# Where the seven-product chain keeps its PSUM banks, which product comes sixth, and when q and k are placed

## The chip, the cores and the metric

The kernel runs on one core of a Trainium2 chip. The metric is the device time of one launch in microseconds (us). The kernel before takes 352.87 us, the median of three runs (352.79 to 353.57). One more execution was taken with the hardware profiler; it has a time of its own, given below.

## The reference

Two stages follow each other. The first is causal attention with a forget gate, for 8 batches and 8 heads of 576 positions with 64 dimensions. The second is a two-layer MLP on the 4608 rows that attention gives, 512 wide, with 2048 hidden units and h - tanh(h) between the layers.

```python
scores = scale * np.matmul(q, k.transpose(0, 1, 3, 2))
cum = np.cumsum(np.log(np.clip(f, 0.0001, 1.0)), axis=-1)
decay = cum[:, :, :, None] - cum[:, :, None, :]
scores = np.where(causal, -1000000000.0, scores + decay)
attn = softmax(scores)                       # over the last axis
x = np.matmul(attn, v)                       # heads side by side: 4608 x 512
h = x @ w_in                                 # 4608 x 2048
out = (h - np.tanh(h)) @ w_out               # 4608 x 512, float32
```

## The kernel before

**Attention.** Batch 0 is done in an order written out by hand. From batch 1 on the work goes pair of heads by pair of heads: pair p is heads 2c and 2c+1 of batch b, with p = 4b + c, and each pair has a *slot*. A slot has seven score tiles, s0 to s6 (`scores`, L338): TensorE writes a tile of transposed scores into one of two PSUM banks of the pool `ps_sc`, ScalarE takes the exponential into SBUF, and from batch 2 on GpSimd sets the masked part to zero. `values` (L371) of the pair before comes behind the second tile of a slot: 30 products with v, then VectorE divides by the row sums into `xn`. `turn` (L389) sends `xn` with two DMA transposes on SyncE's queue into `XR`, which holds the input of the MLP with the hidden dimension on the partitions.

**How q and k come in.** They must stand with the head dimension on the partitions, in `QT` and `KT`, one buffer for even batches and one for odd ones. For batches 1 and 2 the raw rows are loaded as one long transfer for each of q and k (L205; those of batch 2 are issued in slot 4), and TensorE transposes them (`trans`, L236) pair by pair, one slot ahead: the transposes of q behind s0, those of k behind s3. Their PSUM tile has the only bank of the pool `ps_tr` (k of batch 1 is in `ps_m`), and VectorE copies it out. From batch 3 on, GpSimd's queue loads blocks (`load_block`, L92), SyncE's queue turns them by DMA (`turn_block`, L101) into `TQ` and `TK`, and then two more transfers each put the two halves into place (`place`, L105: a = 0 for the even heads, a = 1 for the odd ones). With p0 = 4(b-1), the transposes of q are issued in slot p0, those of k in slot p0+1, the two places of q in slot p0+2 behind s0 and s2, and those of k in slot p0+3 behind s0 and s2. The batch's own first slot is p0+4. The list `LOADS` (L209 to L227) holds all this. SyncE takes its queue in order.

**The MLP.** It works in units of 512 rows, nine in all. `mlp1` (L431) makes the hidden values of a unit in 16 steps: four matmuls of 512 columns into one of three banks of the pool `ps_m`, tanh on ScalarE, the sum on VectorE. Units 0 and 1 then have 16 plain steps of the second layer (`mlp2`). Units 2 to 8 use a scheme with seven half-size products in place of eight (`seven`, L509): 14 steps, each one product of eight matmuls of 256 columns for one half m of the columns. Products 0, 2, 4 and 5 add up in one running sum, called the chain, whose PSUM tile is `cx`. ScalarE copies the chain out behind products 0, 2, 4 and 5 (`keep`, into P1, U2, u3 and ost); products 1, 3 and 6 have tiles of their own and VectorE adds them (`add`, L486) to what was kept; `store` sends four quarters of the unit's output from SyncE's queue. VectorE also makes sums of the hidden values that serve as operands (`sums`, `more_sums`); those for product 6 are emitted in steps 5 and 7.

In units 2 to 5 the products come in their order 0 to 6: product 3 opens the tile `cy` and product 6 adds to the same tile, so that U2 needs one addition. In units 6 to 8 (`spare`) product 6 comes ahead of product 5, in a tile `cw` of its own, and U2 is added to twice. The chain has a bank of `ps_m`, product 1 that of `ps_tr`.

**What sets the order.** All five engines run their instructions in the order in which the program emits them. `slot` (L625) goes through the items of a slot and, after each, emits as many MLP steps as the slot's share `TAKE` has reached by then. In slot 7, where the share is 3, a step comes behind `values`, s4 and s6 instead. One exception is `held` (L616): step 10 of `seven`, which is product 5 on the chain just copied out, waits in units 2 to 5 until enough attention work was emitted since the last step:

```python
    def held():
        fn, _, s = mlp[done[0]]
        return fn is seven and s == 10 and since[0] < 0.85
```

Of the kernel before, what the change touches and what calls it, by code (L numbers as in the profile page):

```python
# [8 lines left out]
FP32 = mybir.dt.float32  # L9
# [8 lines left out]
FAR = 3  # L18
# [4 lines left out]
def kernel(  # L23
# [11 lines left out]
    P = 128  # L35
# [6 lines left out]
    NPAIR = H // 2  # L42
# [8 lines left out]
    UW = 512  # L51
    SB = UW // 2
    NU = NT // UW
# [9 lines left out]
    ps_sc = ctx.enter_context(tc.tile_pool(name="ps_sc", bufs=2, space=PSUM))  # L63
    ps_av = ctx.enter_context(tc.tile_pool(name="ps_av", bufs=1, space=PSUM))
    ps_tr = ctx.enter_context(tc.tile_pool(name="ps_tr", bufs=1, space=PSUM))
    ps_m = ctx.enter_context(tc.tile_pool(name="ps_m", bufs=3, space=PSUM))
# [25 lines left out]
    def load_block(dst, src, b, n, h0=0, h1=H):  # L92
        pn = min(P, S - n * P)
        nc.gpsimd.dma_start(out=dst[0:pn, n, h0:h1, 0:D], in_=src[b, h0:h1, n * P:n * P + pn, :].rearrange("h p d -> p h d"))  # L94
# [10 lines left out]
    def place(dst, src, b, a):  # L105
        nc.sync.dma_start(out=dst[b % 2][0:D, a:H:2, 0:S], in_=src[a * D:(a + 1) * D, :, :])

    def load_v(b, n):
        load_block(vn[b % 2], v, b, n)

    def raw_of(b):
        return 1 if b == FAR else 0
# [46 lines left out]
    def load_aug(b):  # L159
        i, h0 = b % 2, b * H  # L160
        nc.sync.dma_start(out=KT[i][D:D + 1, :, 0:S], in_=chi[h0:h0 + H, :])
        nc.sync.dma_start(out=QT[i][D + 2:D + 3, :, :], in_=cq[h0:h0 + H, :])
        nc.sync.dma_start(out=KT[i][D + 1:D + 2, :, 0:S], in_=clo[h0:h0 + H, :])
# [40 lines left out]
    def load_qk(dst, src, b, h0, h1):  # L204
        nc.gpsimd.dma_start(  # L205
            out=dst[b % 2][:, h0:h1, :, :].rearrange("p h n d -> p h (n d)"),
            in_=src[b, h0:h1, :, :].rearrange("h (p n) d -> p h (n d)", n=NT6))

    LOADS = {(NPAIR, 5): [lambda: load_qk(qn, q, 2, 0, H)],  # L209
             (NPAIR, 6): [lambda: load_qk(kn, k, 2, 0, H)]}  # L210
    for i in range(2 * HF):
        LOADS.setdefault((2 * NPAIR + 3 + i // 4, i % 4 * 2), []).append(lambda i=i: weight_sums(i))
    for b in range(2, B):
        p0 = (b - 1) * NPAIR
        for n in range(NJ):
            LOADS.setdefault((p0 + 1, n), []).append(lambda b=b, n=n: load_v(b, n))
        LOADS.setdefault((p0, 0), []).append(lambda b=b: load_aug(b))
        if b < FAR:
            continue
        for n in range(NJ):  # L220
            LOADS.setdefault((p0 - 1, n), []).append(lambda b=b, n=n: load_block(qb[raw_of(b)], q, b, n))
            LOADS.setdefault((p0, n), []).append(lambda b=b, n=n: load_block(kb[raw_of(b)], k, b, n))
            LOADS.setdefault((p0, 4), []).append(lambda b=b, n=n: turn_block(TQ, qb[raw_of(b)], b, n))
            LOADS.setdefault((p0 + 1, 4), []).append(lambda b=b, n=n: turn_block(TK, kb[raw_of(b)], b, n))
        for n, (dst, src) in enumerate(((QT, TQ), (KT, TK))):
            for a in range(2):
                LOADS.setdefault((p0 + 2 + n, 2 * a), []).append(lambda b=b, dst=dst, src=src, a=a: place(dst, src, b, a))  # L227

    E, XN, GT, M2, AV = {}, {}, {}, {}, {}

# [103 lines left out]
    LAST = 3  # L334
# [130 lines left out]
    CH = {}  # L465
    P1, U2 = (x[:, 0:UW] for x in snap)
# [19 lines left out]
    def add(to, ps):  # L486
        nc.vector.tensor_tensor(out=to, in0=ps, in1=to, op=ALU.add)  # L487
# [4 lines left out]
    def product(u, ph, m, ps, fresh):  # L492
        for ft in range(HF):
            nc.tensor.matmul(out=ps, lhsT=stationary(u, LHS[ph], ft, m), rhs=moving(RHS[ph], ft),  # L494
                             start=fresh and ft == 0, stop=(ft == HF - 1), skip_group_check=True)
# [11 lines left out]
            sums(u, s - 4, 3)  # L507

    def seven(u, s):  # L509
        spare, last = u > NU - 4, u == NU - 1  # L510
        ph, m = divmod(s, 2)
        if spare:
            ph = (0, 1, 2, 3, 4, 6, 5)[ph]
        at = slice(m * SB, (m + 1) * SB)
        if s == 0:
            x = [ps_m.tile([P, UW], FP32, tag="m", name="cx") for _ in range(1 + last)]
            CH["x"] = [(x[0], slice(0, UW))] if not last else [(t[:, 0:SB], slice(i * SB, (i + 1) * SB)) for i, t in enumerate(x)]
        if s == 2:
            CH["z"] = ps_tr.tile([P, UW], FP32, tag="tr", name="cz")
        if s == 6:  # L520
            CH["y"] = ps_m.tile([P, UW], FP32, tag="m", name="cy")
            CH["w"] = ps_sc.tile([P, UW], FP32, tag="sc", name="cw") if spare else CH["y"]
        if ph in (1, 3, 6):
            ps = CH[{1: "z", 3: "y", 6: "w"}[ph]][:, at]
            product(u, ph, m, ps, m == 0 and (ph < 6 or spare))
        else:
            x = CH["x"][m if last else 0][0]
            product(u, ph, m, x if last else x[:, at], ph == 0 and (last or m == 0))
        chain = [CH["x"][m]] if last else CH["x"][0:m]

        def keep(to):
            for x, cols in chain:
                nc.scalar.activation(out=to[:, cols], in_=x, func=AF.Copy)  # L533

        if ph == 0:
            keep(P1)
        if ph == 2:
            keep(U2)
        if ph == 4:
            if s == 8:  # L540
                CH["u3"] = tmp.tile([P, DM], FP32, tag="ost", name="u3")
            keep(CH["u3"])
        if ph == 5 and last:
            ost = tmp.tile([P, DM], FP32, tag="ost", name="ost")[:, 0:SB]
            if m:
                nc.vector.tensor_copy(out=ost, in_=chain[0][0])
            else:
                nc.scalar.activation(out=ost, in_=chain[0][0], func=AF.Copy)
            store(u, 1, 0, ost, m, m + 1)
        elif ph == 5 and m:  # L550
            ost = tmp.tile([P, DM], FP32, tag="ost", name="ost")
            keep(ost)
            store(u, 1, 0, ost)
        if m:
            if ph == 1:
                add(P1, CH["z"])
                store(u, 0, 0, P1)
            if ph == 3 and spare:
                add(U2, CH["y"])
            if ph == 4:  # L560
                add(CH["u3"], CH["y"])
                store(u, 1, 1, CH["u3"])
            if ph == 6:
                add(U2, CH["w"])
                store(u, 0, 1, U2)
        more_sums(u, s)

# [16 lines left out]
    mlp = [(fn, u, s) for u in range(2) for fn in (mlp1, mlp2) for s in range(NFT)]  # L584
    mlp += [(fn, u, s) for u in range(2, NU) for fn, n in ((mlp1, NFT), (seven, 14)) for s in range(n)]
    done = [0]

    def step(n=1):
        for fn, *args in mlp[done[0]:done[0] + n]:
            fn(*args)  # L590
        done[0] += n
# [3 lines left out]
    def att_items(p):  # L595
        items = []
        here = pairs[p] if p < len(pairs) else None
        before = pairs[p - 1] if NPAIR < p else None
        after = pairs[p + 1] if p + 1 < len(pairs) else None
        for ti in range(len(TILES)):  # L600
            if here:
                items.append((lambda ti=ti: scores(*here, ti), "s%d" % ti))
            for load in LOADS.get((p, ti), ()):
                items.append((load, ""))
            if ti == 0 and after and after[0] < FAR:
                items.append((lambda: trans(*after, qn, QT, "AV" if after[0] == 1 else "VV"), "q"))
            if ti == 1 and before:
                items.append((lambda: (values(*before), turn(*before)), "v"))
            if ti == 3 and after and after[0] < FAR:
                items.append((lambda: trans(*after, kn, KT, "VV"), "k"))  # L610
        return items

    goal, since = [0], [0]
    WORK = {"s%d" % LAST: 0.2, "v": 0.9, "q": 0.2, "k": 0.2, "": 0}

    def held():  # L616
        fn, _, s = mlp[done[0]]
        return fn is seven and s == 10 and since[0] < 0.85

    def upto(n):  # L620
        while done[0] < n and (not held() or mlp[done[0]][1] > NU - 4):
            step()
            since[0] = 0

    def slot(p, take):  # L625
        items = att_items(p)
        whole, n, base = sum(c != "" for _, c in items), 0, goal[0]
        for i, (emit, what) in enumerate(items):
            emit()
            since[0] += WORK.get(what, 0.4)  # L630
            if take in FEW and p < 2 * NPAIR:
                if what in FEW[take] and not (what == "s1" and p > NPAIR) or what == "v":
                    step()
                continue
            n += what != ""
            upto(base + n * take // whole)
        goal[0] = base + take
        upto(goal[0])
# [138 lines left out]
```

## Time and profile before

| what | value |
|---|---|
| median of three runs | 352.87 us |
| profiled execution: its own time | 355.07 us |
| its span (first to last instruction) | 353.1 us |
| TensorE busy | 339.1 us |
| VectorE, ScalarE, GpSimd busy | 234.1, 223.1, 150.9 us |
| moved by DMA | 44.66 MB |

In the profile PE is TensorE's matmuls, PEld its weight loads, DVE is VectorE, ACT ScalarE, POOL GpSimd and SP SyncE; a q behind an engine's name means its queue of instructions that are no computation, such as the issue of a DMA. A row of a timeline has the start, the duration, the engine, the line, the operation, the tiles (out<-in), the shape and the number of instructions merged; in square brackets stands how long the engine sat idle just before, and what ended that. The PEclk row is the clock that TensorE was granted. [...]

### The profile page before, as it was taken

What the parts mean: (1) busy time and instruction counts of PE and PEld (TensorE: products, weight loads), DVE (VectorE), ACT (ScalarE), POOL (GpSimd) and SP (SyncE); (2) the same over time, 40 slices, a digit from 0 to 9 for tenths busy, and PEclk for the clock granted to TensorE, in tenths of its full rate; (3) what the DMA queues carried; (4) which work ended last, traced back from release to release, by engine and by line L of the source; (5) the groups of instructions that cost most, each with busy time, mean ns of one, the idle gap of its engine ahead of it and who ended that gap; (6) DMA issues with size and microseconds to landing.
All of it is one profiled execution on the core that took longest, in us unless ns stands there. A gap on an engine that the chain in (4) does not pass through costs nothing.

```text
span 353.1 us, 8789 instructions
## 1 busy us (share of the span) xinstructions
PE 339.1 (96%) x3384; PEld 238.1 (67%) x3384; DVE 234.1 (66%) x475; ACT 223.1 (63%) x417; POOL 150.9 (43%) x291
## 2 busy tenths in 40 slices
PE   7989997999999999999999999899999999999996
PEld 3878885555555557788877567555877787477475
DVE  6487886437963498548844785278628865974973
ACT  4687883457765687558755874688558842633631
POOL 8954622565267635655486547572222220000000
PEclk9999998999999999999999999999999999999999
DMA  9999999999999999999799969999621013002002
GB/s 87 142 198 188 194 173 160 143 143 175 109 129 181 142 157 137 180 150 173 127 185 168 175 103 184 161 180 124 144 86 46 19 48 109 0 31 91 0 32 89
DMA packets 157483, 44.66 MB, mean 126 GB/s; under 512 B 137666, under 2 KB 155394, under 8 KB 157442
## 3 DMA queue, kind: packets, MB, share of 16 engines
q0 software_dynamic: 100128, 18.36, 75.2%
q1 hardware_dynamic: 57234, 25.68, 37.5%
q8 instruction: 26, 0.43, 0.5%
q14 instruction: 15, 0.12, 0.1%
q10 hardware_dynamic: 80, 0.07, 0.1%
HBM read 36.85 MB, written 9.44 MB: 131 GB/s over the span
## 4 chain that ended last, share of the span: by engine, by line
PE 77%; DMA 12%; POOL 5%; DVE 2%; issue 1%; ACT 1%; SPq 0%; POOLq 0%; ACTq 0%
PE hps L453 30%; PE cx L494 13%; PE ps L349 9%; PE ops L574 8%; PE av L377 7%; DMA qn<-in_q_dram 5%; PE cy L494 5%; DMA vn<-in_v_dram 5%; PE cz L494 3%; DMA KT<-TK 2%; PE cw L494 1%; POOL vn L94 1%; POOL kn L98 1%; POOL qn L98 1%; DVE gt L406 1%
## 5 line engine op out<-in xcount | busy, mean ns | idle before, releaser
L453 PE MATMUL hps<-XR,win 128*128 128x512 f16 (+4 forms) x640 | 125.7, 336 | 0.2
L358 ACT ACTIVATE e<-ps 128x512 f16<-128x512 f32 x168 | 98.5, 594 | 42.4 <-PE ps L349 35.9
L406 DVE TENSOR_TENSOR gt<-hps,th 128x512 f16<-128x512 f32 x144 | 98.5, 688 | 29.9 <-ACT th L405 28.8
L405 ACT ACTIVATE th<-hps 128x512 f32<-128x512 f32 x144 | 86.1, 598 | 29.7 <-PE hps L453 20.8
L368 POOL TENSOR_SCALAR_AFFINE_SELECT e<-e 128x128 f16<-128x128 f16 x144 | 49.4, 343 | 103.1 <-ACT e L358 102.6
L453 PEld LDWEIGHTS <-win 128*128 128x128 f16 x640 | 56.3, 97 | 43.7 <-issue 0.5
L349 PE MATMUL ps<-QT,KT 67*128 67x512 f16 (+1 forms) x336 | 69.3, 277 | 4.2 <-DMA KT<-TK 1.7
L494 PEld LDWEIGHTS <-gt 128*128 128x128 f16 x560 | 52.8, 98 | 7.9 <-DVE gt L406 0.4
L349 PEld LDWEIGHTS <-KT 67*128 67x128 f16 x336 | 31.8, 98 | 26.3 <-issue 3.6
L94 POOL DMA_DIRECT2D vn<-in_v_dram x40 | 34.1, 855 | 13.8 <-PE ps L349 3.8
L574 PE MATMUL ops<-wout,gt 128*128 128x512 f16 x128 | 33.3, 385 | 0.0
L377 PEld LDWEIGHTS <-e 128*128 128x128 f16 x784 | 28.8, 98 | 3.3
L377 PE MATMUL av<-vn,e 128*128 128x65 f16 x784 | 29.9, 195 | 0.0
L94 POOL DMA_DIRECT2D qn<-in_q_dram x25 | 21.3, 852 | 11.1 <-DMA wout<-in_moe_w_out_dram 4.2
L385 DVE TENSOR_TENSOR xn<-av,rs 128x640 f16<-128x640 f32 x28 | 23.1, 825 | 1.0
L494 PEld LDWEIGHTS <-sw 128*128 128x128 f16 x224 | 21.1, 97 | 3.9
L383 DVE TENSOR_SCALAR rs<-av 128x10 f32<-128x10 f32 x28 | 4.6, 163 | 27.7 <-PE av L377 27.6
L94 POOL DMA_DIRECT2D kn<-in_k_dram x25 | 21.4, 854 | 1.6 <-issue 1.4
L533 ACT ACTIVATE snap<-cx 128x512 f32<-128x512 f32 (+1 forms) x16 | 8.7, 544 | 16.2 <-PE cx L494 16.2
L574 PEld LDWEIGHTS <-gt 128*128 128x128 f16 x128 | 11.2, 98 | 10.4 <-issue 0.6
L296 ACT ACTIVATE e<-ps 128x512 f16<-128x512 f32 x25 | 14.3, 596 | 5.0 <-PE ps L294 3.0
L487 DVE TENSOR_TENSOR snap<-cy,snap 128x512 f32<-128x512 f32 x7 | 4.8, 690 | 18.4 <-PE cy L494 15.5
(108 smaller groups left out, 412.2 us busy)
## 6 DMA issues: line engine op xcount, KB each, us to landing
vn<-in_v_dram POOLq DMA_DIRECT2D x32, 128.0 KB, 6.0
out_dram<-ost SPq DMA_DIRECT2D x14, 256.0 KB
out_dram<-snap SPq DMA_DIRECT2D x14, 256.0 KB
qn<-in_q_dram POOLq DMA_DIRECT2D x24, 128.0 KB, 5.7
kn<-in_k_dram POOLq DMA_DIRECT2D x24, 128.0 KB, 4.7
QT<-TQ SPq DMA_DIRECT2D x10, 288.0 KB
KT<-TK SPq DMA_DIRECT2D x10, 288.0 KB
win<-in_moe_w_in_dram POOLq DMA_DIRECT2D x2, 1024.0 KB, 13.3
```

The costliest lines, as they stand in the source:

```text
L94: nc.gpsimd.dma_start(out=dst[0:pn, n, h0:h1, 0:D], in_=src[b, h0:h1, n * P:n * P + pn, :].rearrange("h p d -> p h d"))
L296: nc.scalar.activation(out=e, in_=ps, func=AF.Exp, scale=qscale)
L349: nc.tensor.matmul(out=ps[:, col:col + n], lhsT=KT[b % 2][0:D + 3, h, j * P:(j + 1) * P], rhs=QT[b % 2][0:D + 3, h, i0:i0 + n], start=True ...
L358: nc.scalar.activation(out=e[:, lo:hi], in_=ps[:, lo:hi], func=AF.Exp, scale=qscale)
L368: nc.gpsimd.affine_select(out=view, in_=view, compare_op=ALU.is_ge, fill=0.0, base=0, pattern=pat, channel_multiplier=-1)
L377: nc.tensor.matmul(out=av[:, a, ib, :], lhsT=E.pop((b, 2 * c + a, j, ib)), rhs=vn[b % 2][:, j, 2 * c + a, 0:D + 1], start=(j == 0), stop=( ...
L385: nc.vector.tensor_tensor(out=xn.rearrange("p i (a d) -> p a i d", a=2), in0=av[:, :, :, 0:D], in1=rs.to_broadcast([P, 2, NJ, D]), op=ALU. ...
L405: nc.scalar.activation(out=th, in_=hps, func=AF.Tanh, scale=-1.0)
L406: nc.vector.tensor_tensor(out=to, in0=view(hps), in1=view(th), op=ALU.add)
L453: nc.tensor.matmul(out=hps[:, o:o + n], lhsT=win[:, ci, ft * P:(ft + 1) * P], rhs=XR[:, ci, t:t + n], start=(ci == 0), stop=(ci == NCH - 1))
L494: nc.tensor.matmul(out=ps, lhsT=stationary(u, LHS[ph], ft, m), rhs=moving(RHS[ph], ft), start=fresh and ft == 0, stop=(ft == HF - 1), skip ...
L574: nc.tensor.matmul(out=ops, lhsT=GT[(u, ft, m)], rhs=wout[:, ft, :], start=(ft == 0), stop=(ft == NFT - 1))
```

## The change

Four things are done together.

1. In `seven`, the chain `cx` takes the bank of `ps_tr`. Products 1, 3 and 6 each take a bank of `ps_m` in turn. In the last unit, where the chain has two tiles, the second is in `ps_sc`.
2. Product 6 comes ahead of product 5 in all units, and has a tile of its own in all. In units 2 to 5 this adds one addition to U2 in each. `held` goes.
3. The places of q are issued in slot p0+1 behind s5 and s6, those of k in slot p0+2 behind s5 and s6.
4. In slot 7, which holds the transposes of batch 2's first pair, those of q come behind s2 instead of s0, and those of k behind s4 instead of s3 (and behind the MLP step that follows s4).

```diff
         for n, (dst, src) in enumerate(((QT, TQ), (KT, TK))):
             for a in range(2):
-                LOADS.setdefault((p0 + 2 + n, 2 * a), []).append(lambda b=b, dst=dst, src=src, a=a: place(dst, src, b, a))
+                LOADS.setdefault((p0 + 1 + n, 5 + a), []).append(lambda b=b, dst=dst, src=src, a=a: place(dst, src, b, a))
...
     def seven(u, s):
-        spare, last = u > NU - 4, u == NU - 1
+        last = u == NU - 1
         ph, m = divmod(s, 2)
-        if spare:
-            ph = (0, 1, 2, 3, 4, 6, 5)[ph]
+        ph = (0, 1, 2, 3, 4, 6, 5)[ph]
         at = slice(m * SB, (m + 1) * SB)
         if s == 0:
-            x = [ps_m.tile([P, UW], FP32, tag="m", name="cx") for _ in range(1 + last)]
-            CH["x"] = [(x[0], slice(0, UW))] if not last else [(t[:, 0:SB], slice(i * SB, (i + 1) * SB)) for i, t in enumerate(x)]
-        if s == 2:
-            CH["z"] = ps_tr.tile([P, UW], FP32, tag="tr", name="cz")
-        if s == 6:
-            CH["y"] = ps_m.tile([P, UW], FP32, tag="m", name="cy")
-            CH["w"] = ps_sc.tile([P, UW], FP32, tag="sc", name="cw") if spare else CH["y"]
+            x = ps_tr.tile([P, UW], FP32, tag="tr", name="cx")
+            CH["x"] = [(x, slice(0, UW))]
+            if last:
+                x1 = ps_sc.tile([P, UW], FP32, tag="sc", name="cx")
+                CH["x"] = [(t[:, 0:SB], slice(i * SB, (i + 1) * SB)) for i, t in enumerate((x, x1))]
         if ph in (1, 3, 6):
-            ps = CH[{1: "z", 3: "y", 6: "w"}[ph]][:, at]
-            product(u, ph, m, ps, m == 0 and (ph < 6 or spare))
+            if m == 0:
+                CH[ph] = ps_m.tile([P, UW], FP32, tag="m", name="cz")
+            product(u, ph, m, CH[ph][:, at], m == 0)
...
             if ph == 1:
-                add(P1, CH["z"])
+                add(P1, CH[1])
                 store(u, 0, 0, P1)
-            if ph == 3 and spare:
-                add(U2, CH["y"])
+            if ph == 3:
+                add(U2, CH[3])
             if ph == 4:
-                add(CH["u3"], CH["y"])
+                add(CH["u3"], CH[3])
                 store(u, 1, 1, CH["u3"])
             if ph == 6:
-                add(U2, CH["w"])
+                add(U2, CH[6])
                 store(u, 0, 1, U2)
...
-            if ti == 0 and after and after[0] < FAR:
+            late = 2 * (p == 2 * NPAIR - 1)
+            if ti == late and after and after[0] < FAR:
                 items.append((lambda: trans(*after, qn, QT, "AV" if after[0] == 1 else "VV"), "q"))
...
-            if ti == 3 and after and after[0] < FAR:
+            if ti == 3 + late // 2 and after and after[0] < FAR:
                 items.append((lambda: trans(*after, kn, KT, "VV"), "k"))
...
     def upto(n):
-        while done[0] < n and (not held() or mlp[done[0]][1] > NU - 4):
-            step()
-            since[0] = 0
+        step(max(0, n - done[0]))
```

In the two orders of instructions, TensorE has the same number of rows, and VectorE has four additions more. On SyncE's queue three things move for each batch from 3 on: the second place of q goes ahead of a `turn`, both places of k stand together ahead of the next `turn` (the second was behind it), and, in units 2 to 4, the store of U2 goes ahead of the five transposes of the next batch's q, where it was behind them and behind the store of ost. GpSimd's order is unchanged.

More of the change, by code (lines that the diff above doesn't have):

```diff
@@ L608, in att_items @@
                 items.append((lambda: (values(*before), turn(*before)), "v"))
-            if ti == 3 and after and after[0] < FAR:
+            if ti == 3 + late // 2 and after and after[0] < FAR:
                 items.append((lambda: trans(*after, kn, KT, "VV"), "k"))
         return items
[L613 to L618, printed above, removed]
+    goal = [0]
     def upto(n):
-        while done[0] < n and (not held() or mlp[done[0]][1] > NU - 4):
-            step()
-            since[0] = 0
+        step(max(0, n - done[0]))
     def slot(p, take):
@@ L629, in slot @@
             emit()
-            since[0] += WORK.get(what, 0.4)
             if take in FEW and p < 2 * NPAIR:
```

## The prediction

> **What bounds the kernel now.** I read the page's busy rows and slices first.
>
> ```profile
> PE 339.1 (96%) x3384; PEld 238.1 (67%) x3384; DVE 234.1 (66%) x475; ACT 223.1 (63%) x417; POOL 150.9 (43%) x291
> PE   7989997999999999999999999899999999999996
> PEclk9999998999999999999999999999999999999999
> ```
>
> TensorE is the bound: busy 96% of the span, so only its remaining gaps can be won, and the change takes no matmul away. The slices place them: the start, slice 7 (53 to 62 us, where the granted clock dips as well) and slice 26. The table of waits (engine, line, what ended the wait: us in all, times, longest) and the timeline name them.
>
> ```profile
> PE t L245 <- DMA qn<-in_q_dram: 1.9, 1, 1.9
> PE ps L349 <- DMA KT<-TK: 1.7, 2, 1.2
> PE ps L349 <- ACT el L358: 1.7, 3, 0.6
> ```
>
> ```profile
> 57.10 0.43 PE L245 MATMUL t<-id,qn 96*128 96x96 f16 x6 [1.86 <-DMA qn<-in_q_dram]
> 62.21 0.38 PE L349 MATMUL ps<-QT,KT 67*128 67x512 f16 x1 [0.30 <-ACT e L358]
> ...
> 185.42 0.38 PE L349 MATMUL ps<-QT,KT 67*128 67x448 f16 x2 [0.58 <-ACT el L358]
> ...
> 210.59 1.37 SPq L106 DMA_DIRECT2D KT<-TK  x1
> 212.01 2.83 SPq L392 DMA_TRANSPOSE XR<-xn  x1
> 214.89 1.23 SPq L394 DMA_TRANSPOSE XR<-xn  x1
> 216.16 0.60 SPq L106 DMA_DIRECT2D KT<-TK  x1
> 216.85 0.61 PE L349 MATMUL ps<-QT,KT 67*128 67x512 f16 x3 [0.50 <-DMA KT<-TK]
> 222.48 0.42 PE L349 MATMUL ps<-QT,KT 67*128 67x64 f16 x2 [1.25 <-DMA KT<-TK]
> ```
>
> From 55 us on these are nearly all: batch 2's q (1.86), a late exponential (0.30), one wait in each of units 2, 3 and 5 (0.58, same place), and batch 6's two K transfers (0.50 and 1.25, then 0.15 behind the exponential). The third view is busy time and granted clock by stretch.
>
> ```profile
> core 0: us, PE busy (x) PEld busy (x) DVE busy (x) ACT busy (x) POOL busy (x), PEclk, DMA share, GB/s
> 54.15:57.56 3.41, 1.55 (x17) 0.97 (x15) 1.97 (x3) 1.94 (x4) 0.88 (x1) 1.00 1.51 176
> 57.56:60.97 3.41, 3.41 (x37) 2.42 (x36) 2.81 (x5) 0.60 (x1) 0.88 (x1) 0.50 2.98 134
> 221.38:224.79 3.41, 2.16 (x18) 1.63 (x19) 0.69 (x1) 1.86 (x4) 2.53 (x6) 1.00 2.44 151
> ```
>
> After the 1.86 us wait TensorE ran at half clock for 3.41 us. The wait at 222 us, in a stretch that was 63% busy instead of 45%, had no such effect.
>
> **Batch 2's first transposes.** The q load is issued at 38.49 us and takes 18.56 to land: 57.06. The k load is issued at 39.27 and takes 21.4: 60.69. s0 of slot 7 ends at 55.09 in both kernels. At full clock the pieces cost, start to start, 0.37 (s1), 0.90 (`values`), 0.87 (an MLP step), 0.35 (s2), 0.27 (six transposes), 0.12 (s3), 0.27 (s4), 0.63 (s5 and s6). After: 55.09 + 0.37 + 0.90 + 0.87 + 0.35 reaches q at 57.6, behind its landing, so that wait is gone. q ends at 57.9, s3 at 58.0; s4 waits for the exponential of s2 as it does now, 0.85 behind the end of s2, and ends at 58.7; the step ends at 59.6. Then comes k, and k lands only at 60.69: a new wait of 1.1 us. The bank that both share is free by then (q's copies take 1.62 on VectorE and start 0.47 behind the transposes: 59.7). From 60.73: k 0.27, s5 and s6 0.63, step 0.87 to 62.5. The first tile of slot 8 needs the copies of k, 60.73 + 0.47 + 1.62 = 62.85, another 0.35. In the profiled execution that tile starts at 64.83, so 1.98 us are gained. Without the half clock the present order would be at k by 60.0, wait to 60.73 too, and be done 0.27 + 0.27 + 0.87 + 0.63 + 0.87 later, at 63.64: then the gain is 0.79. Both orders hang on the landing of k. I take 1.4, the middle, since three runs within 0.78 us of each other do not say how many of them had the half clock.
>
> **Seventh ahead of sixth, no hold.** Around 185 us the order is s2, step 9, then s3, s4 and s5 in a row (the hold keeps step 10 back), then steps 10 and 11. s5 waits for the bank whose exponential is queued behind the copy of the chain on ScalarE. After, it is s3, step 10, s4, step 11, s5: a step of 0.87 lies between tiles, more than the 0.58 that is missing. Three of these: 1.73 us. Product 5 then follows the chain's copy by two steps (1.75 us), where the copy ends 0.8 us behind step 9. What is added is four additions of 0.69 us on VectorE. In 137 to 154 us it is busy 8.9 of 17 us, so I cost them at nothing. Queued behind the new one (step 7) are the last two sums that step 10 reads, now 0.8 us of work: step 7 ends, 0.2 + 0.69 + 0.8 = 1.7 us pass, and steps 8 and 9 cover 1.75 us plus 0.4 to 1.3 of attention. Unit 6 runs this order now without a gap. Without that cover it would cost at most the addition, 4 x 0.69 = 2.8 us; below nothing it can't go. Of the banks, `ps_m` loses the long-held chain; I find no wait on it now, so nothing is taken for it.
>
> **Places a slot sooner.** Batch 6's second K half is issued at 216.16, behind a `turn` of 2.83 + 1.23 us. After, it follows the first half directly (about 211), 4.9 us sooner, and 1.25 + 0.15 us go. The first half keeps as many issues in front (the second q half passes the earlier `turn` instead), but in the queue its data no longer stand directly behind that q half, so its 0.50 goes too: the trace has that half's packets (of 1152 bytes) from 211.82 to 213.54, 1.7 us, and those of the first K half right behind them, from 213.50. Against this stands the U2 store, now in front of the five turns of q. At 187 SP comes free of u's store at 187.53, U2's addition ends about 187.6, so the turns start 0.65 later; the store behind them (1.39 there) is gone, and by the turns of k SP is level. Adding up its rows, SP issues 32.2 us of the 36.4 from one set of q turns to the next: little room, but the wait it gains is short. The `turn` that q's second half passes is 0.8 later; `XR` is nowhere waited for. TensorE arrives 0.58 sooner, which the 1.7 covers. Gain 1.9; ends 0 (all of it stays) and 1.9.
>
> **Sum.** 1.4 + 1.73 + 1.9 = 5.0 us, or 5.6 with the half clock. In the profiled execution that is 355.07 (353.1 of span and 1.97 around) to 349.5. It stands 2.2 above the median; on the median the sum gives 352.87 - 5.0 = 347.9, and the time should lie in 347.2 to 348.6.
>
> **Rivals.**
> (a) The clock is halved again, now by the wait for k. In 57.56 to 60.97 TensorE would be busy about 1.8 of 3.41 us, 53%, between the 45% that was followed by half clock and the 63% that was not; where the stretches lie against the kernel may shift from run to run. Cost 3.41 / 2 less the 0.35 that the copies hide anyway: 1.35, 349.3. Against it: most positions of the stretch take in more work. [...]
> (b) K stays late. SP is so full that the first half lands no sooner, while TensorE comes 0.58 sooner: 0.5 to 1.9 of the gain go, middle 1.2, about 349.1.
> (c) Slower: the U2 store holds up SP. It waits for the addition behind step 11, on a VectorE that has `xn` and gates queued, and the turns of q, those of k and all four places stand behind it. From about 2.6 us of delay (the 0.65 that costs nothing, the 1.7 of margin and a little) the first tile of slots 20, 24 and 28 waits. At 5 us: 3 x 2.4 = 7.2 lost, only 3.1 won, 357. At 3.6 it is even. For it: 36.4 us of waiting for VectorE on SP's stores (the table of waits). Against: five of them, the longest 17.4 us, at the end where SP has nothing else; U2's addition is never over 0.7 long.
> (d) It does not do what it says: the same exponentials are waited for one tile later, K too, and k swallows what q gains: within 0.5 of 352.9.
>
> **How the numbers follow.** Forecast 0.58, (a) 0.15, (b) 0.13, (d) 0.04, (c) 0.10. Below, 347.2 with 0.7 us for gate waits that could go too (0.15, 0.09) and load times that differ between executions: 346.5. Above, (a) and (b) together, 347.9 + 1.35 + 1.2 = 350.5, and some: 350.9. That leaves out (c), (d) and tails. 0.2% (0.7 us) is about what a measurement of this kernel can tell from no change. Faster: forecast, (a) and (b), 0.86; same 0.03 and slower 0.11 from (d) and (c).
>
> **What would show it.** Right: in the profile after, no wait of TensorE for qn, one of about 1.1 us for kn at the transposes, no half clock at 57 to 61, no wait for the exponential of el in steps 9 to 11, none for KT at slot 24, and SP's K places in pairs. Wrong: half clock after 61, waits for KT at the start of slots 20, 24 or 28 with the U2 store late in front, or product 6's weight loads waiting for VectorE's sums.

## The result and the profile after

The changed kernel is not the 5 us faster that was forecast. Its median over 22 runs is 353.75 us (347.79 to 358.47), against 352.44 us (351.14 to 354.40) for the kernel before. The ratio of the two is 0.9942 with a 95% interval of 0.9914 to 0.9969; that ratio counts only executions within 1.5% of a kernel's fastest, which leaves out 14 of the changed kernel's 22, so the median is given beside it. Two later series of 12 runs gave medians of 354.08 (ratio 0.9955, 0.9910 to 1.0000) and 353.79 (1.0018, 0.9987 to 1.0050). Over the three series, 31 of 46 executions took more than 353 us and 6 took less than 350.2. The change has made the time spread, and no gain is left in the middle of it.

The page of the profiled execution, whose own time is 353.45 us (span 351.7):

```profile
PE 337.3 (96%) x3384; PEld 236.7 (67%) x3384; DVE 236.1 (67%) x479; ACT 222.7 (63%) x417; POOL 150.1 (43%) x291
PE   6989999999999999999999995999999999999995
PEclk9899999999999999999999998999999999999999
```

The dip in the seventh digit is gone, in TensorE's row and in the clock's. The one that was in the 26th digit is now in the 25th and deeper (5 where it was 8), and the clock has one there too. The table of TensorE's waits names it:

```profile
PE ps L349 <- DMA KT<-TK: 5.0, 3, 3.7
```

Rows of the timeline from slot 7, and from slot 23 and the start of slot 24 (issues on SyncE's queue, then TensorE):

```profile
57.41 0.38 PE L349 MATMUL ps<-QT,KT 67*128 67x512 f16 x1 [0.30 <-ACT e L358]
...
58.78 0.41 PE L245 MATMUL t<-id,kn 96*128 96x96 f16 x6
...
60.89 0.39 PE L349 MATMUL ps<-QT,KT 67*128 67x512 f16 x1 [0.22 <-DVE KT L254]
...
202.72 1.38 SPq L106 DMA_DIRECT2D QT<-TQ  x2
204.20 2.55 SPq L392 DMA_TRANSPOSE XR<-xn  x1
206.81 1.22 SPq L394 DMA_TRANSPOSE XR<-xn  x1
208.19 2.26 SPq L106 DMA_DIRECT2D KT<-TK  x2
210.50 1.98 SPq L392 DMA_TRANSPOSE XR<-xn  x1
...
215.51 0.61 PE L349 MATMUL ps<-QT,KT 67*128 67x512 f16 x3 [3.67 <-DMA KT<-TK]
```

In slot 7 the wait for q is gone and k is hardly waited for (0.07 us), and gone are the three waits for the exponential of `el` in the seven products. In their place TensorE waits for K at the first tile of slots 20, 24 and 28: 0.72, 3.67 and 0.66 us, 5.0 in all, where the kernel before lost 1.75 at slot 24 alone. The K places do stand in a pair. The first is issued at 208.19 instead of 210.59, 2.4 us sooner. But TensorE is at that tile at 211.84 instead of 216.35, 4.5 us sooner. What SyncE issued ahead of K in the kernel before:

```profile
205.98 0.69 SPq L106 DMA_DIRECT2D QT<-TQ  x1
206.78 1.51 SPq L392 DMA_TRANSPOSE XR<-xn  x1
208.35 1.39 SPq L394 DMA_TRANSPOSE XR<-xn  x1
209.80 0.63 SPq L106 DMA_DIRECT2D QT<-TQ  x1
```

Busy time and granted clock around the wait at slot 24:

```profile
core 0: us, PE busy (x) PEld busy (x) DVE busy (x) ACT busy (x) POOL busy (x), PEclk, DMA share, GB/s
211.84:215.25 3.41, 0.00 (x1) 0.00 (x0) 0.00 (x0) 0.03 (x1) 0.41 (x1) 1.00 1.94 168
213.40:216.80 3.40, 1.29 (x11) 1.00 (x12) 0.00 (x0) 0.80 (x2) 0.14 (x1) 1.00 1.97 159
216.80:220.20 3.40, 3.40 (x40) 2.89 (x39) 2.68 (x6) 0.28 (x1) 2.19 (x4) 0.50 1.68 195
```

The 3.67 us without work (211.84 to 215.51) are followed, from 216.80 on, by 3.4 us at half clock, a further loss of up to 1.7. In the 3.4 us just ahead of the half clock TensorE was busy 38% of the time (1.29 of 3.40). So the long wait cost over 5 us in this execution (3.67 + 1.7), as much as the gain that was forecast.

### The profile page after: what moved, and what is told of

It is laid out like the page before. It is cut to its first block, busy times and chain, and to the rows that moved or that the text cites. A ratio compares the mean times of both kernels' runs of the same rounds, so it can differ in the third digit from the quotient of the medians.

```text
span 351.7 us, 8795 instructions
## 1 busy us (share of the span) xinstructions
PE 337.3 (96%) x3384; PEld 236.7 (67%) x3384; DVE 236.1 (67%) x479; ACT 222.7 (63%) x417; POOL 150.1 (43%) x291
## 4 chain that ended last, share of the span: by engine, by line
PE 79%; DVE 6%; DMA 6%; ACT 5%; SPq 1%; issue 1%; POOL 0%; ACTq 0%; DVEq 0%
PE hps L453 28%; PE cx L494 11%; PE ps L349 9%; PE cz L494 8%; PE ops L572 8%; PE av L377 7%; DMA KT<-TK 5%; PE hps L439 3%; DVE gt L406 2%; ACT e L358 2%; ACT th L405 2%; PE ps L291 1%; ACT e L296 1%; DVE KT L254 1%; SPq L394 1%
## 5 line engine op out<-in xcount | busy, mean ns | idle before, releaser
L487 DVE TENSOR_TENSOR snap<-cz,snap 128x512 f32<-128x512 f32 x21 | 14.5, 691 | 28.0 <-ACT e L358 12.8
L572 PE MATMUL ops<-wout,gt 128*128 128x512 f16 x128 | 32.5, 378 | 0.0
L494 PE MATMUL cz<-wout,gt 128*128 128x256 f16 x224 | 27.8, 272 | 0.0
```

The costliest lines, as they stand in the source:

```text
L572: nc.tensor.matmul(out=ops, lhsT=GT[(u, ft, m)], rhs=wout[:, ft, :], start=(ft == 0), stop=(ft == NFT - 1))
```

## The experiments

The theories that the expectations name: **A**, the time won on TensorE is real, but K comes at its own pace, so TensorE only arrives sooner and waits; **B**, the store of U2 in front of the transposes holds up the queue; **C**, the moved places make K late; **D**, the new order of the products, with its banks and additions, costs time itself; **E**, added after the first four runs, the DMA engines make K late, because block loads run at the same time.

All series but two have 12 runs (those two have 6). The median of the kernel before was 352.23, 351.98, 352.16 and 352.81 us in the four groups of runs.

| kernel | median us (range) | ratio to before (95%) | KT waits in the profile, us |
|---|---|---|---|
| changed, again | 354.08 (348.46 to 356.58) | 0.9955 (0.9910, 1.0000) | 2.6 |
| places back | 350.50 (349.93 to 353.63) | 0.9971 (0.9947, 0.9995) | 4.4 |
| U2 store back | 354.76 (351.16 to 356.15) | 1.0055 (1.0025, 1.0085) | 3.5 |
| seven products undone | 351.52 (349.97 to 357.47) | 0.9979 (0.9949, 1.0009) | 0.9 |
| seven products alone | 351.96 (350.09 to 356.79) | 0.9992 (0.9961, 1.0022) | 2.6 |
| K places right behind q's | 350.10 (346.80 to 352.92) | 0.9924 (0.9891, 0.9957) | none; XR 3.1 |
| places on ScalarE's queue | 352.05 (350.31 to 356.67) | 1.0004 (0.9971, 1.0038) | 0.3, and see below |
| no q loads for batches 5 to 7 | 348.16 (347.37 to 348.88) | 0.9881 (0.9850, 0.9913) | 0.6 |
| q loads a slot sooner | 349.21 (348.05 to 350.14) | 0.9889 (0.9842, 0.9937) | 1.4 |
| sooner, K behind q | 352.39 (349.58 to 354.00) | 0.9990 (0.9956, 1.0025) | none; XR 3.0 |
| before, no q loads | 350.11 (349.41 to 352.10) | 0.9923 (0.9890, 0.9955) | none |
| sooner, places back | 350.26 (348.27 to 351.26) | 0.9941 (0.9909, 0.9972) | 1.8 |
| before, q loads sooner | 351.44 (350.63 to 353.62) | 0.9970 (0.9945, 0.9995) | 0.6 |
| q loads sooner, again | 350.54 (348.73 to 353.15) | 0.9931 (0.9902, 0.9960) | 3.6 |
| changed, third | 353.79 (350.92 to 359.24) | 1.0018 (0.9987, 1.0050) | 0.8; XR 1.3 |

### The changed kernel again

> The changed kernel once more, unedited, beside the other runs, so that they are compared on one chip and so that a second profile shows which of its waits differ from one execution to the next. Theory A (the time won on TensorE up to slot 24 is real, about 4.5 us, but the K transfers of batches 5 to 7 come through SyncE's queue and the DMA rings at their own pace, so TensorE only arrives sooner at the first tile of slots 20, 24 and 28 and waits there): 349 to 355 us, with the differences between executions in the waits for KT and in one stretch of half clock (1.7 us) that follows a long one. Theory D (something else, such as the four additions or the banks, costs time): the waits for KT are alike in all executions and the difference lies elsewhere.

The time fell as theory A has it, and this profile (span 350.9) is one without a half clock (mean clock 1.000). Its waits of TensorE:

```profile
PE ps L349 <- DMA KT<-TK: 2.6, 2, 2.1
...
PE ps L349 <- ACT snap L531: 1.4, 1, 1.4
```

2.1 us at slot 24, 0.5 at slot 28, and 1.4 at the first tile of slot 16. That last wait stands under ScalarE's name, but it was K as well: the first K half of that batch landed at 142.12 us, 0.09 ahead of the tile, and the copy named had ended at 141.49. The K waits thus differ between executions in size and in slot, and are there in quick executions too.

### Each part undone, or alone

The U2 store back behind the transposes:

```diff
                 add(U2, CH[6])
-                store(u, 0, 1, U2)
+            if s == 13:
+                store(u, 0, 1, U2)
```

> The changed kernel with the store of U2 issued in step 13 behind the store of ost, as before, instead of in step 11 ahead of the five transposes of q; the addition itself stays in step 11. Theory A: within 1 us of the changed kernel, since SyncE gains about 0.6 us and gives it back behind the transposes. Theory B (the store in front of the transposes holds up the whole chain of turns and places): the KT waits fall from 5.0 us to under 2, no half clock follows, and the time is 348 to 350 us.

Theory B falls: 0.7 us above the changed kernel on the same chip (354.08), which is within the noise, with a KT wait of 3.5 us at slot 24 in the profile. The store in front of the turns is not the cause.

The places back:

```diff
-                LOADS.setdefault((p0 + 1 + n, 5 + a), [])...
+                LOADS.setdefault((p0 + 2 + n, 2 * a), [])...
```

> The changed kernel with the places of q and k where they were before (behind s0 and s2 of slots p0+2 and p0+3); all else changed. Theory A: the first K half is issued at about the same time and the second some 5 us later, so TensorE waits for both: the sum of the KT waits grows from 5.0 to 6 or more, and the time is 1 to 3 us above the changed kernel's. Theory C (moving the second q half and the second K half ahead of the turns is what makes the first K half late): the first K half lands 1 to 2 us sooner against TensorE, the wait at slot 24 falls to 2 us or less, and the time is 1 to 3 us below the changed kernel's.

The direction is not theory A's: the median is 3.6 us below that of the changed kernel on the same chip (354.08). The ratios to the kernel before, 0.9971 and 0.9955, do not show it; the mean clocks do: here none of 12 executions is under 0.993, there 6 of 12 are at 0.990 or less. But neither did K come sooner, as theory C wants. The packets of batch 6's first K half end at 214.46 us, in the first profile of the changed kernel at 214.49, and TensorE goes on at 215.50 and 215.51. The profile shows what is different:

```profile
PE ps L349 <- DMA KT<-TK: 4.4, 5, 1.6
```

The same K time is waited for in five pieces, none over 1.6 us, and the clock stays at full speed (mean 1.000). In the changed kernel slot 20 has little wait (0.72 us), so slot 24 takes it in one piece (3.67), and the half clock comes on top. The executions of the changed kernel agree: over its three series, those with a mean clock of 0.997 or more have a median of 351.36 us (9 of 46), those at 0.9925 or less, which I estimate to be two stretches of half clock or more (the profile of the kernel before has one and a mean of 0.995, that of the changed kernel two, one of them at the start, and 0.990), 354.99 (23 of 46). Of the 35 executions of the kernel before on this chip, two are at 0.9925 or less.

The seven products undone, which leaves the places and batch 2's transposes:

```diff
 # the kernel before, with
+                LOADS.setdefault((p0 + 1 + n, 5 + a), [])...
+            late = 2 * (p == 2 * NPAIR - 1)
```

> The kernel before with only two parts of the change: the places a slot sooner and batch 2's first transposes later; the seven products with their banks, their order and the hold are as before. Theory A: slot 7 gains 2 to 4 us, the three waits of 0.58 stay, and TensorE arrives at slot 24 only some 3 us sooner instead of 4.5, so the KT waits stay under 3 us: 349 to 352 us, less spread than the changed kernel. Theory B: no KT wait over 0.7 us, because the U2 store is behind the transposes again: 348 to 350 us.

As theory A expected, 0.9 us of KT wait; the waits of 0.58 are there, four of them. And the seven products alone:

```diff
 # the changed kernel, with
+                LOADS.setdefault((p0 + 2 + n, 2 * a), [])...
+            late = 0
```

> The kernel before with the seven-product part alone: banks, order, no hold; the places and batch 2's first transposes stand as before. Theory A (TensorE's gains are real, the K transfers come at their own pace): slot 7 keeps its wait for q and mostly its half clock, the three waits of 0.58 are gone, and of these 1.7 us about half comes back as longer KT waits at slot 24 (2 to 3 us in all there): 351 to 353 us. If the seven-product part itself cost time (theory D), slots without a batch's start would be longer than before and the time 353 us or more with the KT waits as before.

351.96, as much as the kernel before. The profile, one of its quicker executions (350.42 us), shows where a part of its gain went:

```profile
PE ps L349 <- DMA KT<-TK: 2.6, 5, 0.9
PE t L245 <- DMA qn<-in_q_dram: 0.6, 1, 0.6
PE t L245 <- DMA kn<-in_k_dram: 0.5, 1, 0.5
```

The waits of 0.58 are gone, and the waiting for K is 2.6 us, where the kernel before had 1.75. Slot 7 has no half clock here, against the expectation (mean clock 0.999). Each of these two alone is within the noise of the kernel before; together their median is worse.

### What makes K late: the queue or the DMA engines

K's places ahead of one more turn:

```diff
-                LOADS.setdefault((p0 + 1 + n, 5 + a), [])...
+                LOADS.setdefault((p0 + 1, 5 + n), [])...
```

> The changed kernel with the places of k issued right behind those of q, in slot p0+1, so that they stand ahead of one more turn in SyncE's queue: 4 us sooner by the durations in the profile after (2.55 + 1.22 us for that turn). Theory A in the form 'the queue in front of K is what is late': the KT waits at slots 20, 24 and 28 are gone or under 0.5 us, no half clock behind slot 24, 346 to 348.5 us. In the form 'the DMA engines are what is late' (theory E): K lands at best 1 to 2 us sooner, 2 us of waiting stay, 350 to 353 us.

No wait for K is left, but there is a new long one, and the mean clock is 0.995:

```profile
PE hps L453 <- DMA XR<-xn: 3.1, 1, 3.1
```

What was put in front of the turns is in time, and the turns, whose output the next unit of the MLP needs, are late instead. This execution, 352.92 us, is the slowest of its 12; their median is 1.9 us better than before, above the 346 to 348.5 of the queue form. So the place in the queue does decide who waits.

All places on another queue:

```diff
-        nc.sync.dma_start(out=dst[b % 2][0:D, a:H:2, 0:S], ...)
+        nc.scalar.dma_start(out=dst[b % 2][0:D, a:H:2, 0:S], ...)
...
-                LOADS.setdefault((p0 + 1 + n, 5 + a), [])...
+                LOADS.setdefault((p0 + 2 + n, 2 + a), [])...
```

> The changed kernel with all four places on ScalarE's queue, those of q in slot p0+2 behind s2 and s3, those of k in slot p0+3 behind s2 and s3: later in the program, but behind no turn. Theory A in the queue form: the first K half is issued within 0.5 us of its place in the program, its packets follow within 1.5 us, and the KT waits are under 1 us; ScalarE loses some 0.6 us per place where its exponentials have room: 347 to 350 us. Theory E: packets take as long as in the changed kernel (3.8 us from issue to the first) and 2 us or more of waiting stay.

Issue was no longer the trouble: ScalarE issued batch 6's K halves at 209.18 and 209.91, and no turn was in front of them. Their first packet follows 1.8 us behind the issue, not 3.8 as theory E has it. Yet their packets ran from 211.0 to 216.6 us, 5.6 us for two halves of 288 KB, and the first tile of slot 24 waited 0.95 us at 214.97. The trace puts that wait down to an exponential that was long done; the first half landed at 214.88. So K is slow with no turn in front of it too, and the median, 352.05, is that of the kernel before.

The loads taken away:

```diff
+            if b < 5:
                 LOADS.setdefault((p0 - 1, n), []).append(... load_block(qb[raw_of(b)], q, b, n))
```

> The changed kernel without the block loads of q for batches 5, 6 and 7 (25% of the loads in that part; the transposes and places of q still run, on what the buffer holds, so those batches' outputs are not attention of their q). These loads run at the very time of the K places. Theory E (the DMA engines' load makes K late): the KT waits shrink to under 1 us, 347 to 349.5 us. Theory A in the queue form: SyncE's queue is as full as before, so K lands at most 1 us sooner and 2 us or more of waiting stay.

Theory E holds. 348.16 us, and all six runs within 1.5 us of each other. SyncE issues both K halves at 206.73, 1.5 us sooner:

```profile
206.73 1.84 SPq L106 DMA_DIRECT2D KT<-TK  x2
208.61 2.53 SPq L393 DMA_TRANSPOSE XR<-xn  x1
```

Here is the stretch from 208 to 212 us in the table by stretches, without the loads and then in the changed kernel:

```profile
208.00:212.00 4.00, 3.94 (x36) 3.03 (x34) 1.84 (x5) 2.76 (x6) 0.99 (x3) 1.00 0.82 178
```

```profile
208.00:212.00 4.00, 3.84 (x35) 3.00 (x32) 2.23 (x5) 2.28 (x4) 3.60 (x8) 1.00 1.77 75
```

The last two columns are the time that packets took, as a share of the 16 DMA engines' time (over 1 where several are open at once on an engine), and the rate. The two stretches do not hold the same traffic. Without the loads it is mostly K: the packets of both halves run from 208.57 to 211.73, the first 1.8 us behind its issue. In the changed kernel, where K was issued at 208.19, the stretch holds almost only the loads, in packets of 128 bytes; K's first packet starts at 212.02, 3.8 us behind its issue, and its last ends at 217.78. By queue (packets, MB, share of the 16 engines' time), from 204 to 212 us in the changed kernel; q0 is GpSimd's, with the loads:

```profile
q0 software_dynamic: 2040, 0.26, 176.3%
q1 hardware_dynamic: 1107, 0.73, 63.3%
```

The loads carry a quarter of the bytes and take nearly three quarters of the packets' time. From K's issue to the first tile of slot 24 it is 7.3 us in the changed kernel (208.19 to 215.51), 5.8 with the places on ScalarE's queue (209.18 to 214.97) and 4.2 without the loads (206.73 to 210.96). The loads are slower in the changed kernel, too. Their time from issue to landing (the last column, us) there, and then in the kernel before, in the same 8 us against TensorE:

```profile
qn<-in_q_dram POOLq DMA_DIRECT2D x4, 128.0 KB, 8.4
```

```profile
qn<-in_q_dram POOLq DMA_DIRECT2D x4, 128.0 KB, 6.4
```

### The loads at another time, and what the change is worth then

Nothing left out; q's loads for batches 5 to 7 go to the one slot of four that has none:

```diff
-                LOADS.setdefault((p0 - 1, n), []).append(... load_block(qb[raw_of(b)], q, b, n))
+                LOADS.setdefault((p0 - 1 - (b > 4), n), []).append(... load_block(qb[raw_of(b)], q, b, n))
```

> The changed kernel with the block loads of q for batches 5, 6 and 7 one slot sooner (p0-2 instead of p0-1), into the one slot of four that has no loads; nothing is left out. If it is the meeting of these loads with the K places that makes K late (theory E), most of what leaving them out won comes here too: the first K half's packets within 2 us of its issue, KT waits under 1 us, 347.5 to 350 us, close together. If it is the sum of the loads (theory E'), K stays 2 us or more late: 352 to 354.5 us.

> The changed kernel with the same sooner loads, once more, on the same chip as the two others: 348 to 350.5 us, and 1 to 2 us below the kernel before with that edit.

This is below the kernel before on two chips, 349.21 and 350.54 us, with ratios of 0.9889 (0.9842 to 0.9937) and 0.9931 (0.9902 to 0.9960), and on the second chip 3.25 us below the changed kernel (353.79). It is the meeting in time, not only the sum of the loads. The waits are shorter, not gone; in the two profiles:

```profile
PE ps L349 <- DMA KT<-TK: 1.4, 2, 0.8
```

```profile
PE ps L349 <- DMA KT<-TK: 3.6, 3, 1.4
```

None is over 1.4 us, and there is no half clock behind them (mean clock 1.000 in both). On the second chip the sum was 3.6 us, where less than 1 was expected, and the time just above its range.

> The same with the places of k right behind those of q as well. Theory E: K is early in any case; the turn of the last pair of a batch, which then was 3.1 us late for the next unit, is no longer held up by the q loads, so its wait (XR) goes as well: 347 to 349 us. If the turns are late for SyncE's queue alone, the XR wait stays at 1 us or more in some executions: 349 to 351 us.

> The changed kernel with q's block loads one slot sooner and the places where they were before. Theory E: the first K half is early enough (waits under 0.7 us), the second stays behind one more turn (0 to 1 us at s3): 348 to 350.5 us, at most 1 us from the same kernel with the places moved. If the places matter by themselves once the loads are out of the way, it is 1.5 us or more slower than that one.

K right behind q costs here: 3.0 us of waits for XR in two places, and 352.39 us, above both ranges. The turns are late with the q loads out of the way, too; theory E was wrong on this point. (The profile has 3.3 us of waits for q and k up to slot 7 besides.) With the places back where they were, 350.26, 1.05 above the moved places on the same chip (12 runs against 6): about what was expected, though slot 24 waits 1.4 us for the first K half, not under 0.7.

> The kernel before without the block loads of q for batches 5, 6 and 7 (the same loads left out as from the changed kernel, which then took 348.16). What lies between the two is what the change is worth when the transfers are not in the way. Theory A with E: the KT waits of the kernel before go too (1.75 us), the three waits of 0.58 and slot 7 stay, so 350.3 to 351.5 us, 2.1 to 3.3 above. Theory D (the changed seven products cost time of their own): 349 us or less, under 1 us apart.

> The kernel before with q's block loads for batches 5 to 7 one slot sooner, nothing else. Theory E: the loads' meeting with the K places cost the kernel before only the 1.75 us that its profile shows in KT waits, so 350.3 to 351.5 us; with the changed kernel's 349.2 for the same edit, the change is worth 1 to 2 us once the loads are out of the way. If instead the sooner loads are what wins and the change adds nothing, this kernel is at 349.5 us or less.

> The changed kernel, unedited, on the same chip: 351 to 355 us in most executions, a few below 350, 3 to 5 us above the one with sooner loads; where the profile has a KT wait of over 3 us at slot 24, half clock behind it.

With the loads left out, the kernel before takes 350.11 and the changed one 348.16: 1.95 us apart (2.1 to 3.3 were expected), and no execution of the one lies within the range of the other. With the loads sooner, on one chip, 351.44 and 350.54: 0.9 apart (1 to 2 expected), hardly clear of the noise, since the two intervals in the table overlap. There the unchanged pair stands at 352.81 and 353.79, the other way round. The waits of TensorE in the kernel before without the loads:

```profile
PE ps L350 <- ACT el L359: 2.3, 4, 0.6
```

Four waits of 0.58 (unit 4's, too, now that K does not hide it) and no KT. These are gone in the changed kernel. The last profile of the changed kernel also has the wait for k in slot 7 that the prediction foretold:

```profile
61.36 0.43 PE L245 MATMUL t<-id,kn 96*128 96x96 f16 x6 [1.50 <-DMA kn<-in_k_dram]
```

## Why the prediction was wrong

**The step that failed is "Places a slot sooner", its gain of 1.9 us.** It set TensorE's earlier arrival at 0.58 us, against a margin of 1.7. It left out that all that is won ahead of slot 24 makes TensorE come sooner: 4.5 us in the profile. It took for granted that the SyncE queue moves up with TensorE and that K's packets follow their issue no later than before. Neither held. The first half was issued only 2.4 us sooner; of the missing 2.1 us, 0.86 came with the pairing itself: the turn behind two places in a row took 2.55 + 1.22 us where it had taken 1.51 + 1.39 behind one, and from the first q half's issue to K's it was 5.47 us instead of 4.61. Then K's first packet came 3.8 us behind the issue instead of 2.9 (212.02, and 213.50 before), and the packets ended only 1.8 us sooner (214.49 against 216.29). The DMA engines carry q's loads just then, which the step doesn't mention; without those loads the delay behind the issue is 1.8. In this pair of profiles the term was not +1.9 but 1.75 - 5.0 = -3.3 us, and with the half clock behind the wait about -5. In the medians, the changed kernel with the places alone put back is 3.6 us faster (350.50 against 354.08).

**Rival (b) was the right mechanism with the wrong size.** It let K take back at most the gain of its own step. A transfer that sets its own time can take back every gain ahead of it, on whatever step that was made: here TensorE came 4.5 us sooner and the packets of the first K half ended 1.8 sooner. Together with (a)'s half clock, at another place than (a) put it, that makes a loss. Where (a) did put it, the profile of the changed kernel with a long wait for k (1.50 us) was 59% busy in 57.00 to 61.40 (2.60 of 4.40 us) and kept the full clock (1.00). **Rival (c)**, the U2 store, was wrong: with the store back the time was no better. **Rival (d)**, no change, is nearest by the median, but not by its account: the exponentials of `el` are no longer waited for.

**Seven products: right.** The waits of 0.58 behind `el` are gone in every profile with the new order (the one where ScalarE issues the places has one of 0.36 elsewhere), and no wait points to the additions or to the sums of product 6. The 1.73 us of waits went as forecast (2.3 in profiles where unit 4 has one, too), but in the time they show only where K does not take them back.

**Batch 2's transposes: the mechanism was right, the size wrong.** In the three profiles of the changed kernel q is not waited for; k, the new wait, cost 0.07 us in two of them and 1.50 in the third (1.1 forecast), the copies of k 0.22 (0.35), the exponential 0.30 (0.46). But the wait of 1.86 with its half clock was not the usual case: in other profiles with the old order of slot 7 the q wait is 0.58, 0.83 or none, and there is no half clock behind it. From the first tile of slot 7 to the first of slot 8 the old order took 10.02 us with the half clock and 6.57, 7.37 and 7.56 without it; the new order took 7.05 to 9.37 in thirteen profiles, in most of them 7.06. So without the half clock the new order gained some 0.3 us, if anything: even the lower end, 0.79, was too high, and I took 1.4. The waits of 0.30 and 0.22 that come with it take back a part of what it saves.

**The range.** 346.5 to 350.9 came from one execution's transfers. The changed kernel alone lies between 347.8 and 359.2.

## What to carry to other kernels

When an engine with hardly a gap is made faster, look first at the transfers that it now waits for a little, at every place, and reckon with its whole advance, not with the last step's. A wait that is split over several places can be cheaper than the same wait in one piece: here 4.4 us in five pieces left the full clock (mean 1.000), and 3.67 in one was followed by 3.41 us of half clock. Where a transfer is late, check what else the DMA engines carry just then before you move it in its queue: here moving it made another transfer late (XR, a wait of 3.1 us), and moving the other load won (349.21 us, ratio 0.9889).

## What the runs showed of the hardware

- The same 288 KB place took 1.8 us of packets with the q loads left out (208.57 to 210.37) and 2.5 with them (212.02 to 214.49), and its first packet came 1.8 and 3.8 us behind its issue. On ScalarE's own queue, with the loads, two of them took 5.6 us, beginning 1.8 us behind the issue.
- SyncE's issue of a DMA transpose took 1.25 us or less in 62 of 106 cases (kernel before) and 69 of 106 (changed kernel). The first one behind a single place of q took 1.5 to 1.6 us (kernel before), behind two places of q in a row 2.3 to 2.6 in four of five cases (changed kernel), and 2.4 to 2.5 in four of five with the q loads left out. Behind a single place of k it took 1.2 to 2.8 us with the q loads and 1.2 to 1.3 without (kernel before). So in these runs a second place in front and the loads each went with a longer issue behind; the prediction counted on neither.
- Stretches of half clock, as the profiles show them: 3.41 us in the kernel before (57.56 to 60.97), twice 3.41 us in the changed kernel (8.57 to 11.98 and 216.78 to 220.19). In the 3.41 us ahead of each TensorE was busy 45% (1.55 us), 65% (2.20) and 38% (1.29 of 3.40, in the table above). Stretches of that length that were followed by full clock were busy 55% (changed kernel, 1.88 us from 209.96 to 213.37) and 63% (kernel before, 2.16 us from 221.38 to 224.79). So neither the wait nor the busy share alone tells the two apart over these runs: a wait of 1.86 us was followed by half clock and one of 2.12 was not (changed, again, mean clock 1.000), and 65% was followed by it at the start where 55% in mid-kernel was not. What decides it was not shown.
